# A new order table for a 16-token-tile adaLN linear-attention and MLP block on one core

## The chip, the cores and the metric

The kernel runs on one core of one Trainium2 chip. The metric is the time of one execution on the device in microseconds (us); the median of several executions is given. Engines are named as the profile names them: PE is TensorE's matmul, PEld its weight load, DVE is VectorE, ACT is ScalarE, POOL is GpSimd, and SP is SyncE, whose queue issues nearly all the DMAs here.

## The reference

There are 2048 tokens of width 576, 32 heads of width 18, and an MLP of width 4608. All arrays are float32.

```python
mod = (silu(c) @ w_mod)                      # six rows of 576: sa, ca, ga, sb, cb, gb
h = layernorm(x) * (1 + ca) + sa
q, k, v = h @ wqkv                           # per head
phi = lambda t: where(t > 0, t + 1, exp(t)) + 1e-6
kv, z = sum_s phi(k) v, sum_s phi(k)         # over all tokens
o = phi(q) kv / (phi(q) z + 1e-6)
x = x + ga * (o @ wo)
h = layernorm(x) * (1 + cb) + sb
out = x + gb * (silu(h @ w1) @ w2)
```

## The kernel before

The tokens lie in 16 tiles of 128, in four blocks of four. Every matmul operand is kept as a rounded part and a rest ("hi" and "lo"), so that a product takes three matmuls instead of one: hi times hi, lo times hi, hi times lo. ScalarE makes the hi part as a copy (`w_hi`, `split_h`, `scaled_hi`), and VectorE makes the rest as a difference of two tiles in SBUF (`sub_hi` on L262, `scaled_lo` on L268). This is why VectorE and GpSimd have so much to do.

The program has these stages, each with its span in the profile:

- **First projections** (0 to about 24 us): the modulation row from `c`, and K of the first two token tiles.
- **K and Q** (24 to about 210 us): for each block of four tiles LayerNorm, the transposed and modulated activations `hT` (rest parts on L262 for the first block and L998 for the others), K and phi(K) (`psK`, L929), partial products with the rows of x (`psG`, L1054; VectorE adds them into `sum` on L1064), Q for most tiles, and the second and third part of the modulation rows (GpSimd sums `tmod`, L1104). Then the state `kv` and its product with `wo` (L1224).
- **Attention output and the second LayerNorm** (210 to about 357 us): `big`, L390 and L1358; the transposes of the normalised rows into `small` (L375) and their hi and lo parts; beside it a first MLP slice in a plain form, `small` L1433 up and `big` L1444 down, whose results VectorE adds into the output rows `acc` (L1449).
- **MLP** (357 to the end): the remaining slices, in which seven products replace eight (a Strassen scheme over 2x2 blocks of tokens, hidden columns and outputs). An up product (`up`, L1925) is taken out of PSUM by VectorE on L1947 and L1949 and by ScalarE, GpSimd forms sums and differences of the results (L1960 to L1967), hi and lo parts are made (L1983, L1987), and the down products (`down`, L2009) are added to `acc` and to helper rows `U` by VectorE (L2018 to L2022). The weights are prepared in the same way: GpSimd sums (L1575 to L1583), hi parts, lo parts (L262, L268).

How the order of the work is set: the code first writes down the operations stage by stage (`STAGE_A` orders the K and Q stage while it is written down; the rest of the MLP is written down by the small scheduler `Schedule.emit`). At the end, `arrange(ORDERS, begun)` (L252, called on L2380) goes through the table `ORDERS`, which has one list of numbers for each engine. Number n is the n-th instruction that was written down for that engine after `begun`; the list says in which order the engine runs them, and each instruction is tied to the one before it in the list. What is not in a list follows in the order in which it was written. The lists hold the first 2991 of the 6939 matmuls and transposes, 656 instructions of VectorE, 486 of ScalarE, 258 of GpSimd and 203 DMAs on SP's queue. This covers the program until about 470 us of the profile; the steady part of the MLP behind it is in no list.

An engine runs its list strictly in order: when one instruction waits, all behind it wait too. The waits themselves come from the data and from buffers that are used again. A PSUM bank can be written again only when VectorE or ScalarE has read it out.

```python
ORDERS = {                                   # L67
    "PE": """ 0-43 45-46 52 49-50 ... """, "DVE": ..., "Activation": ..., "Pool": ..., "SP": ...
}
def arrange(orders, start):                  # L252
    for engine, text in orders.items():
        traced = [i for i in nc.cur_bb.bb.instructions[start:] if i.engine == ... and listed(i)]
        order = [j for part in text.split() for j in span(part)]
        order += sorted(set(range(len(traced))) - set(order))
        for a, b in zip(order, order[1:]):
            follow(traced[b], traced[a])
```

Of the kernel before, what the change touches and what calls it, by code (L numbers as in the profile page):

```python
# [24 lines left out]
def kernel(ctx: ExitStack, tc, A_x, A_wqkv, A_wo, B_x, B_w1, B_w2, c, w_mod, out):  # L25
# [33 lines left out]
    def behind(instructions):  # L59

        with ExitStack() as order:
# [8 lines left out]
            116 84-87 90-91 124 88-89 92-105 117 106-111 125 118-123 112-115 126-141 154-173 142-147 174-177  # L70
            148-153 210-217 178-179 246-249 180-181 250-251 290-291 182-201 218-221 256-267 274-289 202-209
            292-295 302-319 222-227 320-329 228-237 268-273 330-331 296-299 332-335 300-301 336-337 238-245
            252-255 342-343 338-341 344-353 366-367 354-365 368-391 412-413 398-403 392-395 414-423 396-397
            406-411 424-425 436-439 426-427 440-445 404-405 446-451 428-435 452-457 462-463 458-461 464-517
            524-527 518-519 530-533 520-523 534-553 572-573 586-587 574-575 554-571 588-591 598-601 528-529
            592-595 602-609 596-597 610-629 576-579 630-645 580-585 646-653 658-661 682-685 662-669 686-687
            692-697 688-689 698-701 654-657 670-673 690-691 702-703 674-681 704-763 770-771 764-769 772-787
            826-829 788-825 838-843 862-865 830-833 844-845 866-867 846-857 872-875 834-837 890-891 876-877
            892-893 878-889 894-901 858-861 868-871 926-931 902-925 932-943 950-951 944-945 952-963 946-949
            978-983 1000-1001 966-977 984-999 1002-1015 1022-1027 1016-1021 1028-1029 964-965 1030-1075  # L80
            1084-1085 1076-1077 1102-1117 1086-1093 1130-1135 1118-1119 1078-1079 1120-1121 1136-1137 1122-1129
            1138-1139 1080-1083 1140-1145 1094-1095 1160-1161 1096-1101 1146-1157 1172-1177 1162-1171 1158-1159
            1248-1249 1178-1183 1250-1253 1184-1185 1254-1257 1186-1199 1208-1213 1258-1259 1285-1286 1200-1207
            1287-1292 1214-1219 1236-1237 1220-1227 1238-1247 1228-1235 1293-1300 1260-1284 1301-1339 1352-1356
            1340-1351 1357-1386 1413-1417 1387-1412 1418-1439 1446-1450 1440-1445 1451-1488 1507-1510 1489-1494
            1511-1513 1495-1506 1514-1558 1573-1576 1601-1604 1559-1572 1605 1577-1586 1634 1638 1587-1600
            1606-1623 1646-1649 1624-1625 1650 1655-1660 1626-1633 1661-1670 1639 1635-1637 1640-1641 1687-1688
            1671-1678 1715-1719 1679-1680 1642-1643 1681-1682 1651 1689-1694 1652-1653 1644-1645 1695-1698 1654
            1699-1710 1720-1727 1711-1712 1728-1731 1713-1714 1683 1748 1684-1685 1732-1745 1749 1686 1746-1747
            1776-1779 1781-1784 1780 1762 1785-1790 1763-1765 1791-1792 1750 1793-1798 1751-1761 1766-1771  # L90
            1799-1802 1772-1775 1854 1803-1809 1821-1825 1870 1810 1855-1857 1811 1826-1827 1812-1813 1871-1873
            1828-1831 1874-1876 1832-1835 1877 1836-1839 1814-1816 1858-1860 1883-1886 1817-1819 1861-1862 1820
            1840-1843 1863-1864 1844-1853 1865-1868 1915-1918 1869 1878-1882 1887-1904 1976 1990 1977-1980
            1919-1921 1905-1906 1922-1926 1991 1981 1907-1908 1931-1934 1982 1909-1914 1983-1984 1927-1930 1985
            1935 1992 1936-1941 1986 1942-1947 1987-1989 1948-1967 1993-1995 1968-1972 2004-2010 1973-1975
            2011-2022 1996-1999 2023-2028 2000 2029-2036 2001-2003 2037-2038 2049-2069 2039-2048 2070-2081 2086
            2082 2098-2099 2087-2088 2106-2110 2089-2095 2100-2101 2083-2085 2096-2097 2115-2136 2102 2137-2142
            2147 2159-2160 2103-2105 2111-2113 2161-2162 2148 2114 2187-2190 2163-2166 2149 2143-2146 2167-2168
            2150 2169-2186 2151 2191 2199 2192-2194 2200-2202 2152-2153 2203-2210 2195 2213 2211-2212 2154-2158
            2196-2198 2214-2224 2231-2234 2225-2230 2239 2249 2259-2261 2240 2235-2238 2262 2245 2241-2242  # L100
            2246-2247 2243 2255-2258 2248 2244 2265-2270 2295 2263 2250-2254 2271 2264 2272-2274 2296-2298
            2283-2284 2299-2305 2285-2287 2309 2288-2291 2277-2278 2292-2293 2310-2311 2275-2276 2312-2313 2294
            2306-2308 2279-2282 2314-2323 2329-2333 2335 2324 2336-2339 2334 2347-2352 2340 2353-2354 2325-2328
            2355-2358 2341 2359-2363 2342 2364-2365 2343-2344 2366-2369 2345-2346 2370-2375 2377 2376 2378-2382
            2391-2398 2383-2387 2399 2388-2389 2400-2402 2390 2403-2407 2427-2428 2408-2412 2421 2433 2413-2420
# [2306 lines left out]
```

## Time and profile before

| | us |
|---|---|
| median of 3 runs (lowest, highest) | 1093.39 (1093.04, 1094.13) |
| the profiled execution, its own time | 1092.31 |
| span of the profile, first to last instruction | 1090.6 |
| PE busy in the span | 1064.8 (98%) |
| DVE busy | 913.4 (84%) |
| POOL busy | 741.3 (68%) |
| ACT busy | 708.5 (65%) |

The profiled execution took 1.7 us more than its span, and 1.08 us less than the median. A busy PE is a PE with a matmul in flight; idle time of the other engines costs nothing where PE doesn't wait for them. So what matters is where PE is idle, and which engine ends each wait.

### The profile page before, as it was taken

The numbers are of one execution on the slowest core, as the hardware profiler recorded it, in microseconds if no ns is written. First come the engines' busy times: TensorE is split into PE (matmuls) and PEld (weight loads), VectorE is DVE, ScalarE is ACT, GpSimd is POOL, SyncE is SP. The second block draws the span as 40 slices with busy tenths as digits, with TensorE's granted clock in tenths as the row PEclk, the third lists the DMA queues.
The fourth block names the chain that finished last, engine by engine and source line by source line (L and its number), as shares of the span: only waits on it lengthen the run. The fifth ranks groups of instructions, "written<-read, shape, count | busy, mean of one in ns | idle before, by whom it ended". The sixth has DMA issues, their size and how long they took to land.

```text
span 1090.6 us, 19057 instructions
## 1 busy us (share of the span) xinstructions
PE 1064.8 (98%) x7027; PEld 758.6 (70%) x7027; DVE 913.4 (84%) x1438; ACT 708.5 (65%) x1318; POOL 741.3 (68%) x804
## 2 busy tenths in 40 slices
PE   8899999999999899999999999999999999999998
PEld 6899999899785455666666666666666666666665
DVE  7968968778889799998997888987987887898767
ACT  5766554246757686677667767776776776676554
POOL 3556615655725499879878778877788678677563
PEclk9999999999999999999999999999999999999999
DMA  9497665223256768478577667567657747616522
GB/s 292 123 214 174 64 182 130 54 81 106 66 183 224 206 239 249 136 229 247 176 204 244 172 194 224 197 207 221 201 168 254 206 137 264 208 63 201 169 79 109
DMA packets 119342, 193.51 MB, mean 177 GB/s; under 512 B 42892, under 2 KB 77584, under 8 KB 119248
## 3 DMA queue, kind: packets, MB, share of 16 engines
q1 hardware_dynamic: 86276, 190.81, 56.2%
q10 hardware_dynamic: 32972, 1.48, 3.1%
q8 instruction: 55, 0.90, 0.3%
q14 instruction: 39, 0.32, 0.1%
HBM read 176.77 MB, written 15.48 MB: 176 GB/s over the span
## 4 chain that ended last, share of the span: by engine, by line
PE 77%; DVE 12%; ACT 3%; DMA 3%; issue 3%; POOL 2%; SPq 0%; DVEq 0%; POOLq 0%; ACTq 0%
PE up L1925 30%; PE down L2009 29%; PE big L390 6%; PE psK L929 4%; PE psG L1054 3%; DVE hT L262 1%; PE small L1433 1%; PE big L1444 1%; PE psK L1224 1%; DVE acc L1021 1%; DMA hT<-in_B_w_dram 1%; DMA turned<-acc 1%; PE big L1358 1%; DVE w L262 1%; DMA hT<-in_w_mod_dram 1%
## 5 line engine op out<-in xcount | busy, mean ns | idle before, releaser
L1925 PE MATMUL up<-hT,w 128*128 128x512 f16 x1264 | 317.6, 379 | 2.6 <-ACT p L1900 1.6
L1925 PEld LDWEIGHTS <-w 128*128 128x128 f16 x1492 | 146.0, 98 | 140.0 <-issue 3.9
L2018 DVE SCALAR_TENSOR_TENSOR acc<-acc,set,down 128x576 f32<-128x576 f32 x128 | 103.4, 810 | 31.4 <-PE down L2009 30.5
L1943 ACT ACTIVATE f<-f,set 128x512 f32<-128x512 f32 x102 | 73.0, 718 | 59.7 <-DVE f L1949 50.4
L1963 POOL TENSOR_TENSOR s<-f,f 128x256 f32<-128x256 f32 x66 | 55.2, 836 | 73.2 <-ACT f L1944 70.8
L2009 PE MATMUL down<-w,hc 128*128 128x288 f16 x600 | 90.8, 286 | 0.4 <-ACT f L1939 0.4
L2009 PE MATMUL down<-w,hb 128*128 128x288 f16 x600 | 90.5, 286 | 0.2 <-DVE acc L2018 0.2
L2009 PE MATMUL down<-w,hT 128*128 128x288 f16 x480 | 82.9, 286 | 0.4 <-DVE acc L2022 0.4
L1947 DVE TENSOR_TENSOR f<-up,p 128x512 f32<-128x512 f32 x102 | 69.6, 682 | 15.1 <-PE up L1925 8.6
L1944 ACT ACTIVATE f<-f,set 128x512 f32<-128x512 f32 x102 | 73.6, 722 | 3.2
L2009 PEld LDWEIGHTS <-hb 128*128 128x128 f16 x600 | 58.7, 98 | 22.6 <-issue 0.7
L2009 PEld LDWEIGHTS <-hc 128*128 128x128 f16 x600 | 58.6, 98 | 22.5 <-DVE acc L2018 0.7
L1949 DVE TENSOR_TENSOR f<-up,f 128x512 f32<-128x512 f32 x68 | 46.9, 689 | 26.6 <-PE up L1925 25.5
L1987 POOL TENSOR_TENSOR hc<-s,hc 128x512 f16<-128x512 f32 x50 | 63.7, 1274 | 6.4 <-ACT hc L1983 6.4
L1967 POOL TENSOR_TENSOR f<-f,s 128x256 f32<-128x256 f32 x66 | 53.6, 812 | 18.5 <-DVE hb L1987 10.2
L1960 POOL TENSOR_TENSOR s<-f 128x256 f32<-128x256 f32 x66 | 55.9, 847 | 14.1 <-ACT f L1940 11.3
L2009 PEld LDWEIGHTS <-hT 128*128 128x128 f16 x480 | 46.9, 98 | 26.6 <-issue 0.8
L390 PE MATMUL big<-w,qT 128*128 128x288 f32 x352 | 59.6, 307 | 0.6 <-DVE acc L1372 0.6
L1965 POOL TENSOR_TENSOR s<-s,f 128x256 f32<-128x256 f32 x66 | 56.4, 854 | 3.6
L2009 PE MATMUL down<-w,ha 128*128 128x288 f16 x396 | 55.6, 286 | 0.3 <-DVE w L262 0.3
L2009 PE MATMUL down<-w,hd 128*128 128x288 f16 x396 | 55.5, 286 | 0.2 <-ACT hd L1983 0.2
L1987 POOL TENSOR_TENSOR hd<-s,hd 128x256 f16<-128x256 f32 x66 | 50.5, 765 | 6.6 <-ACT hd L1983 6.6
(408 smaller groups left out, 2830.1 us busy)
## 6 DMA issues: line engine op xcount, KB each, us to landing
hT<-hd SPq DMA_DIRECT2D x101, 640.0 KB, 5.2
hT<-hd SPq DMA_DIRECT2D x65, 512.0 KB, 3.9
hT<-in_B_w_dram SPq DMA_DIRECT2D x14, 576.0 KB, 5.1
hT<-in_B_w_dram SPq DMA_DIRECT2D x28, 256.0 KB, 6.4
raw<-in_B_w_dram SPq DMA_DIRECT2D x11, 576.0 KB, 4.4
v<-in_B_w_dram SPq DMA_DIRECT2D x9, 576.0 KB, 5.1
acc<-in_A_x_dram SPq DMA_DIRECT2D x16, 288.0 KB, 5.0
raw<-in_B_w_dram SPq DMA_DIRECT2D x9, 512.0 KB, 5.6
```

Source lines behind the costliest of these rows:

```text
L390: T.matmul(ps, xpart(a), wpart(b), start=n == 0, stop=n == len(XW) - 1)
L1925: T.matmul(ps, left, right, start=first and m == 0, stop=m == len(seq) - 1, skip_group_check=True)
L1943: A.activation(f, f, AF.Silu, scale=factor(self.g, "inv"))
L1944: A.activation(f, f, AF.Identity, scale=factor(self.g, "delta"))
L1947: V.tensor_add(f, self.bank[bank[1]], self.p1)
L1960: G.tensor_sub(self.s3, half(i, 0, 0), half(i, 0, 1))
L1963: G.tensor_add(self.s[:, 0:1], half(i, 0, 1), half(i, 1, 1))
L1965: G.tensor_sub(self.s[:, 1:2], self.s[:, 0:1], half(i, 0, 0))
L1967: G.tensor_sub(half(i, 1, 0), half(i, 1, 0), self.s[:, 1:2])
L1987: eng.tensor_sub(t[:, :, 1, :], src, t[:, :, 0, :])
L2009: T.matmul(ps[:, p, :HALF], left[:, u, p * P : (p + 1) * P], right[:, v], start=n in (1, 5, 7, 6) and j == 0, stop=j == len(passes) - 1, s ...
L2018: V.scalar_tensor_tensor(dst, dst, factor(self.g, "ratio"), ps[:, :, :HALF], op0=ALU.mult, op1=ALU.add)
```

## The change

The diff replaces the five lists of `ORDERS` by five other lists over the same numbers (ScalarE's list takes in three instructions more, GpSimd's four). Nothing else is touched: the same instructions with the same operands run on the same engines, and the tables of `STAGE_A` and the scheduler are as before. [...] The changed file has one line less in the table, so that in its listings every line number behind the table is lower by one (L998 of before is L997).

The first two rows of PE's list, cut to their beginning, show how the table reads:

```diff
     ORDERS = {
         "PE": """
             0-43 45-46 52 49-50 44 47-48 53-54 51 65 57-58 61-62 66-72 55-56 59-60 63-64 73-77 82-83 80-81 78-79
-            116 84-87 90-91 124 88-89 92-105 117 106-111 125 118-123 112-115 126-141 154-173 142-147 174-177
+            84-87 90-91 88-89 92-101 116-118 102-103 124 104-105 119-123 125 106-115 126-141 154-167 142-153
...
```

Up to its 84th instruction PE runs as before (until 24.9 us of the profile). Of the 6939 instructions of PE 2536 stand at another place, of VectorE's 543 of 1438, of ScalarE's 392, of GpSimd's 227 and of SP's 161. Most moves are short: the farthest ones on PE are 64 places forward and 77 back. Behind the lists the order of all engines is the same. Three places show what moved.

VectorE between 99 and 116 us of the profile, where it makes the rest parts `hT` of the third block from the block's rows in `acc_93` and `h_119` (L998; L362 modulates them first), and adds a partial product into `sum_109` (L1064). Before:

```order
L1064 TENSOR_TENSOR sum_108<-psG_116,sum_108 128x576
L942 TENSOR_SCALAR acc_92<-psK 128x576
L495 SCALAR_TENSOR_TENSOR acc_92<-e,acc_92 128x576
L362 TENSOR_SCALAR acc_93<-acc_93,col_a 128x512 x2
L1064 TENSOR_TENSOR sum_109<-psG_117,sum_109 128x576
L998 TENSOR_TENSOR hT<-acc_93,hT 128x4x4x32 x2
L942 TENSOR_SCALAR acc_92<-psK 128x576
L998 TENSOR_TENSOR hT<-acc_93,hT 128x4x4x32
L337 BN_STATS st<-acc_94 128x6 x2
L998 TENSOR_TENSOR hT<-h_119,hT 128x4x4x32
L998 TENSOR_TENSOR hT<-acc_93,hT 128x4x4x32
```

The same stretch of VectorE's instructions in the changed kernel:

```order
L1063 TENSOR_TENSOR sum_108<-psG_116,sum_108 128x576
L1063 TENSOR_TENSOR sum_107<-psG_117,sum_107 128x576
L336 BN_STATS st<-acc_94 128x6 x2
L337 BN_AGGR mv<-st 128x2
L336 BN_STATS st<-acc_94 128x6
L941 TENSOR_SCALAR acc_92<-psK 128x576 x2
L361 TENSOR_SCALAR acc_93<-acc_93,col_a 128x512
L997 TENSOR_TENSOR hT<-acc_93,hT 128x4x4x32
L361 TENSOR_SCALAR acc_93<-acc_93,col_a 128x512
L1063 TENSOR_TENSOR sum_109<-psG_117,sum_109 128x576
L336 BN_STATS st<-acc_94 128x6 x2
L997 TENSOR_TENSOR hT<-acc_93,hT 128x4x4x32 x3
```

The statistics of the next block (BN_STATS, one input) moved ahead; the first addition of L495 and the rest part of `h_119` moved behind the last three of the four parts from `acc_93`.

VectorE at the end of the attention stage, 354 to 361 us: the four additions of the last plain down products (`big`, each with its own bank number) into `acc3`, between weight splits (`w_3657`) and the activations `S`. Before:

```order
L1449 SCALAR_TENSOR_TENSOR acc3_94<-acc3_94,set0_99,big_3888 128x576
L262 TENSOR_TENSOR S_3672<-S_3670,S_3672 128x512
L1449 SCALAR_TENSOR_TENSOR acc3_94<-acc3_94,set0_99,big_3895 128x576
L262 TENSOR_TENSOR S_3672<-S_3670,S_3672 128x512
L268 SCALAR_TENSOR_TENSOR w_3657<-v_3658,set0_99,w_3657 128x256
L1449 SCALAR_TENSOR_TENSOR acc3_94<-acc3_94,set0_99,big_3923 128x576
L268 SCALAR_TENSOR_TENSOR w_3657<-raw_3660,set0_99,w_3657 128x256
L1449 SCALAR_TENSOR_TENSOR acc3_94<-acc3_94,set0_99,big_3881 128x576
L268 SCALAR_TENSOR_TENSOR w_3657<-v_3658,set0_99,w_3657 128x256 x2
L268 SCALAR_TENSOR_TENSOR w_3657<-raw_3660,set0_99,w_3657 128x256
```

The same place in the changed kernel:

```order
L1448 SCALAR_TENSOR_TENSOR acc3_94<-acc3_94,set0_99,big_3888 128x576
L261 TENSOR_TENSOR S_3672<-S_3670,S_3672 128x512
L267 SCALAR_TENSOR_TENSOR w_3657<-v_3658,set0_99,w_3657 128x256
L1448 SCALAR_TENSOR_TENSOR acc3_94<-acc3_94,set0_99,big_3881 128x576
L1448 SCALAR_TENSOR_TENSOR acc3_94<-acc3_94,set0_99,big_3895 128x576
L267 SCALAR_TENSOR_TENSOR w_3657<-raw_3660,set0_99,w_3657 128x256
L1448 SCALAR_TENSOR_TENSOR acc3_94<-acc3_94,set0_99,big_3923 128x576
L267 SCALAR_TENSOR_TENSOR w_3657<-raw_3660,set0_99,w_3657 128x256
```

The addition of `big_3881`, last of the four before, is now the second; the first up product of the MLP waits for it before, and for the addition of `big_3895` in the changed kernel. The two splits of `w_3657` that stood behind the four additions now stand ahead of these rows.

VectorE at about 435 to 441 us, in the MLP, where `w22`, `w24` and `w27` are the rest parts of a weight slice for the down products, `hb0` and `hb1` those of two activations, and `f01` an up product. Before:

```order
L1987 TENSOR_TENSOR hb0_4087<-f01_4633,hb0_4087 128x2x256
L262 TENSOR_TENSOR w24_3971<-S_3808,w24_3971 128x288
L748 TENSOR_TENSOR set1_100<-set1_100,set0_99 128x1
L2018 SCALAR_TENSOR_TENSOR U0_3978<-U0_3978,set1_100,down_4772 128x576
L262 TENSOR_TENSOR w22_3970<-v_3658,w22_3970 128x288
L262 TENSOR_TENSOR w27_3969<-S_3808,w27_3969 128x288
L2022 TENSOR_TENSOR acc3_94<-down_4688,acc3_94 128x2x288
L262 TENSOR_TENSOR w27_3969<-v_3658,w27_3969 128x288
L262 TENSOR_TENSOR w22_3970<-raw_3982,w22_3970 128x288
L1987 TENSOR_TENSOR hb1_4064<-f11_4673,hb1_4064 128x2x256
L1947 TENSOR_TENSOR f01_4853<-up_4791,p1_4788 128x512
```

The same place in the changed kernel:

```order
L1946 TENSOR_TENSOR f10_4755<-up_4589,p1_4586 128x512
L1986 TENSOR_TENSOR hb0_4087<-f01_4633,hb0_4087 128x2x256
L2017 SCALAR_TENSOR_TENSOR U0_3978<-U0_3978,set1_100,down_4772 128x576
L261 TENSOR_TENSOR w22_3970<-raw_3982,w22_3970 128x288
L261 TENSOR_TENSOR w27_3969<-v_3658,w27_3969 128x288
L261 TENSOR_TENSOR w27_3969<-S_3808,w27_3969 128x288
L1946 TENSOR_TENSOR f01_4853<-up_4791,p1_4788 128x512
L1986 TENSOR_TENSOR hb1_4064<-f11_4673,hb1_4064 128x2x256
L2021 TENSOR_TENSOR acc3_94<-down_4688,acc3_94 128x2x288
```

The second half of `w22` moved ahead of two other weight splits and of the addition into `acc3`. On PE, the products that read it moved ahead too: of what PE runs before the fifth of them, 19 up products with `w`, one with `wta` and 12 down products with `hd` now come behind it.

More of the change, by code (lines that the diff above doesn't have):

```diff
@@ L74 @@
[L74 to L88, printed above, removed]
```

198 lines of the change are left out of this document (106 added, 92 removed).

## The prediction

> **What bounds the kernel now.** I first read the busy times of the engines on the page:
>
> ```profile
> PE 1064.8 (98%) x7027; PEld 758.6 (70%) x7027; DVE 913.4 (84%) x1438; ACT 708.5 (65%) x1318; POOL 741.3 (68%) x804
> ```
>
> PE is in use for 98% of the span, so an order can give back at most PE's idle time. Where that lies is read from the busy times by stretch; the stretches are cut where PE's idleness changes (columns: stretch, its length, busy us and instructions of PE, PEld, DVE, ACT, POOL, granted clock, DMA).
>
> ```profile
> 0.00:24.00 24.00, 20.24 (x123) 15.82 (x123) 17.09 (x46) 11.14 (x22) 8.99 (x13) 1.00 0.94 303
> 24.00:60.00 36.00, 32.31 (x236) 31.31 (x237) 31.69 (x51) 28.58 (x45) 18.61 (x15) 1.00 0.49 138
> 60.00:100.00 40.00, 40.00 (x302) 40.00 (x302) 28.74 (x46) 25.18 (x36) 21.73 (x16) 1.00 0.99 200
> 100.00:126.00 26.00, 22.73 (x166) 21.86 (x165) 24.83 (x34) 15.02 (x23) 19.32 (x13) 1.00 0.35 107
> 126.00:170.00 44.00, 43.51 (x328) 43.24 (x327) 32.39 (x42) 26.60 (x46) 14.30 (x10) 1.00 0.81 140
> 170.00:210.00 40.00, 38.71 (x268) 36.01 (x268) 29.75 (x47) 10.39 (x17) 22.91 (x19) 1.00 0.33 82
> 210.00:270.00 60.00, 60.00 (x457) 58.76 (x456) 48.53 (x101) 32.10 (x52) 35.30 (x34) 1.00 0.32 92
> 270.00:300.00 30.00, 28.14 (x195) 22.45 (x194) 26.95 (x41) 22.28 (x37) 22.04 (x19) 1.00 0.31 84
> 300.00:340.00 40.00, 39.72 (x288) 32.27 (x288) 35.91 (x75) 24.56 (x40) 13.30 (x14) 1.00 0.55 189
> 340.00:378.00 38.00, 33.77 (x183) 17.76 (x182) 31.82 (x47) 24.59 (x48) 15.12 (x16) 0.96 0.70 220
> 378.00:410.00 32.00, 31.01 (x187) 18.00 (x185) 30.37 (x45) 26.68 (x56) 29.93 (x37) 1.00 0.68 239
> 410.00:470.00 60.00, 58.43 (x362) 34.63 (x360) 58.90 (x91) 41.05 (x86) 51.28 (x63) 1.00 0.60 182
> 470.00:1050.00 580.00, 580.00 (x3702) 361.98 (x3701) 488.46 (x741) 399.75 (x788) 446.19 (x521) 1.00 0.63 197
> 1050.00:1090.60 40.60, 36.18 (x254) 24.52 (x251) 28.00 (x43) 20.54 (x33) 22.30 (x21) 1.00 0.27 101
> ```
>
> Length less PE's busy time gives the idle time. From 470 to 1050 us there is none, so whatever the lists gain or lose is fixed by about 470 us and carried to the end. The first 24 us (3.76 idle) and the last 40.6 us (4.42) are outside the lists. Between lie 3.69 + 0 + 3.27 + 0.49 + 1.29 + 0 + 1.86 + 0.28 + 4.23 + 0.99 + 1.57 = 17.67 us of idle time: the whole prize. Where PE idles, VectorE is almost always the engine near its limit (24.83 of 26 us, 26.95 of 30, 30.37 of 32, 58.90 of 60).
>
> Second, what holds VectorE up. Durations of one form, as minimum, median and maximum in ns:
>
> ```profile
> L1947 DVE TENSOR_TENSOR f<-up,p x102: 672/678/692, 364.2 to 1072.4; 128x512 f32<-128x512 f32 x102
> L998 DVE TENSOR_TENSOR hT<-acc,hT x12: 678/691/1956, 69.3 to 153.5; 128x512 fp32r<-128x512 f32 x12
> ```
>
> L1947 reads one operand from PSUM and is the same each time, L998 reads two tiles in SBUF and takes up to 1.28 us more for the same work. At 100 to 116 us the two engines stand side by side like this (start, us):
>
> ```profile
> 101.46 1.20 DVE L495 SCALAR_TENSOR_TENSOR acc<-e,acc 128x576 f32<-128x576 f32 x1
> ...
> 106.38 3.08 DVE L998 TENSOR_TENSOR hT<-acc,hT 128x512 fp32r<-128x512 f32 x2
> 110.05 1.96 DVE L998 TENSOR_TENSOR hT<-acc,hT 128x512 fp32r<-128x512 f32 x1
> 112.65 2.42 DVE L998 TENSOR_TENSOR hT<-h,hT 128x512 fp32r<-128x512 f32 x1
> 115.00 0.68 DVE L998 TENSOR_TENSOR hT<-acc,hT 128x512 fp32r<-128x512 f32 x1
> 115.60 0.45 DVE L337 BATCH_NORM_STATS2 st<-acc 128x6 f32<-128x288 f32 x1
> ...
> 102.12 3.39 POOL L1104 TENSOR_TENSOR tmod<-tmod,acc 128x576 f32<-128x576 f32 x2
> 110.02 3.27 POOL L1104 TENSOR_TENSOR tmod<-tmod,raw 64x576 f32<-64x576 f32 x2 [1.11 <-issue]
> ```
>
> The L998 issued at 110.05, beside GpSimd's pair, ends at 112.0: some 0.7 us, its clean time, after the first of the pair (half of 3.27) is done. The one at 112.65, while the second still runs, takes 2.42. So with two operands in SBUF VectorE waits for GpSimd's turn to end. [...]
>
> **The change part by part.** Nothing is added or removed, so each term is a place where a wait of PE gets longer or shorter. I count the work that stands ahead of the instruction that ends a wait, and the PE work ahead of the one that waits, in both orders.
>
> *100 to 126 us (3.27 idle).* Two waits make up most of it:
>
> ```profile
> PE psK L929 <- DVE hT L998: 1.6, 1, 1.6
> PE psG L1054 <- DVE sum L1064: 1.3, 1, 1.3
> ```
>
> The first ends with the L998 at 115.00. In the changed order two of the rows above leave its front, the addition on L495 (1.20) and the part of `h_119` (2.42), 3.6 us as they ran; three statistics and an aggregate take their place, 3 x 0.45 and at most as much again, so 1.4 to 1.8 us is won. PE's work ahead of the one that waits grows by two matmuls, 0.13 us each (302 in 40.00 us from 60 to 100). So the L998 comes about 2 us earlier than now, if the conflicts that left are not replaced; the wait of 1.6 would be gone. For the second wait the sum on L1064 gets the three statistics, one more L998 (0.68) and one more L942 ahead of it and loses the L495: some 2 us of clean work more. PE has 24 more matmuls to run before it needs the sum, 3.1 us, so that stays covered. I take half of the two waits and a little: they hang on conflicts that only partly go. **Taken: -1.7**; bounds -3.3 (both waits go) and +1.7 (the conflicts only change partners and the sum is late).
>
> *340 to 378 us (4.23 idle).* The largest single wait:
>
> ```profile
> 359.70 4.44 PE L1925 MATMUL up<-first,w 128*128 128x512 f16 x12 [2.08 <-ACT S L1632]
> 357.66 0.81 DVE L1449 SCALAR_TENSOR_TENSOR acc<-acc,set,big 128x576 f32<-128x576 f32 x1 [0.31 <-PE big L1444]
> 358.39 0.48 DVE L268 SCALAR_TENSOR_TENSOR w<-raw,set,w 128x256 f16<-128x256 f32 x1
> 358.79 0.81 DVE L1449 SCALAR_TENSOR_TENSOR acc<-acc,set,big 128x576 f32<-128x576 f32 x1
> 360.00:363.00 3.00, 3.00 (x9) 1.08 (x8) 0.79 (x2) 0.28 (x1) 1.69 (x2) 0.50 0.57 171
> ```
>
> The profile names ScalarE, but its `S` was done; by time the fourth addition of L1449, which ends at 359.60 and frees the bank, lets PE go 0.10 later. In the changed order PE waits for the third of the four; the fourth and one split (0.81 + 0.48) come behind it, but two splits (0.9) were pulled ahead of it, so VectorE reaches it only some 0.3 us sooner. VectorE has no slack here (0.31 idle in the rows), so I take 0.3, not the 2.1 of the wait. Right behind the wait the clock stood at 0.50 and twelve matmuls took 4.44 us instead of 12 x 0.216 = 2.6 (rows of the chain of waits further down), a further 1.8 us. With a shorter gap that may go; I count 0.8 for it. **Taken: -1.1**; bounds -4.2 - 1.8 = -6.0, and +1.0 (the first reading of `up` on L1947 now has two `S` differences ahead of it that were behind it, each like the 0.68 of L998 above). [...]
>
> *24 to 60, 126 to 210 and 270 to 340 us* (3.69 + 0.49 + 1.29 + 1.86 + 0.28 = 7.61 idle). The same kinds of instructions are shuffled over at most some tens of places; I found no such clear removal. I take a quarter, half of the share taken at 100 us: **-1.9**; bounds -7.6 and +3.2 (at 50 us PE's products for the second K pair were moved 3.4 us ahead, VectorE's rest part for them 1.1 us back, with 1.3 us between them now).
>
> *378 to 470 us (2.56 idle).* VectorE and GpSimd together have 89.27 + 81.21 us of busy time in 92 us. At 440 us:
>
> ```profile
> 436.27 0.45 DVE L262 TENSOR_TENSOR w<-S,w 128x288 f16<-128x288 f32 x1
> 436.64 0.75 DVE L2022 TENSOR_TENSOR acc<-down,acc 128x576 f32<-128x576 f32 x1
> ...
> 438.60 0.98 DVE L262 TENSOR_TENSOR w<-raw,w 128x288 f16<-128x288 f32 x1
> 440.29 1.14 PE L2009 MATMUL down<-w,hb 128*128 128x288 f16 x8
> ```
>
> What PE's products cost is read from the chain of waits (start, us, what):
>
> ```profile
> 445.01 1.74 PE up L1925 x8
> ...
> 477.43 1.47 PE down L2009 x12
> ```
>
> That is 0.216 us for an up product and 0.122 for a down product. PE's product at 440.29 follows VectorE's split, which ends at 439.58, by 0.7 us. The new lists take 20 up products and 12 down products from in front of it, 5.8 us, but from in front of the split only three others (0.45 each), one addition (0.75), with four tiny steps added: 1.2 us. If VectorE went on at its pace, PE would wait 5.8 - 1.2 - 0.7 = 3.9 us. It will not be quite that if VectorE loses less to GpSimd until there. **Taken: 0**; bounds -2.6 and +3.2 (3.9, less 0.7 us for such waits as PE has behind 440 us now, an estimate: a share of the 1.57 from 410 to 470).
>
> *60 to 100 and 210 to 270 us*: PE is never idle, 0. SP's queue:
>
> ```profile
> 354.00 2.74 DMA hd<-S
> hT<-hd SPq DMA_DIRECT2D x101, 640.0 KB, 5.2
> ```
>
> The fetch of `first` for that first up product moved behind two stores of `hd`. These wait for an `S` of VectorE, and one went out at 354.00. Issued then, the fetch lands at 359.2, 0.5 before PE starts now: 0, while VectorE is no later.
>
> The sum is -1.7 - 1.1 - 1.9 + 0 = -4.7 us. The profiled execution took 1092.31 (span 1090.6 and 1.7 around it), 1.08 below the median; it goes to 1087.6, and the median from 1093.39 to **1088.7**.
>
> **The rivals.** (1) *The MLP's start waits for VectorE.* [...] It decides when VectorE's overrun between 378 and 440 us falls by less than the 3.9 - 0.7 = 3.2 us. With the earlier gains at 0 the time is 1093.4 + 3.2 = 1096.6. For it: 58.90 of 60; against: earlier gains, if any, arrive as slack. (2) *More of it works*: two thirds of the idle time goes, 0.67 x 17.7 = 11.8: 1081.6. For it: every large wait but ScalarE's ends in VectorE, with overrun ahead. (3) *The conflicts only change places*, and the orders are equal on the chip: 1093.4. [...] (4) *The first K tiles get out of step*: +3.2 at 50 us, with nothing back: 1096.6, the same side as (1).
>
> **How the numbers follow.** Forecast 0.40, (1) 0.27, (2) 0.15, (3) 0.12, (4) 0.06. Faster by over 0.2% (2.2 us, about what a measurement of this kernel can tell from no change): 0.40 + 0.15 = 0.55; within: 0.12; slower: 0.33. The range goes from 1077 (most of the prize of 17.7 and some of the clock's 1.8 us) to 1100 (both slower rivals together, 3.2 + 3.2). The forecast's own range is 1083 to 1091.
>
> **What would show it.** Right: between 100 and 116 us the last L997 part ends some 2 us earlier against PE's work and PE's wait for it is under 0.5 us; the wait before the first `up` is under 2 us and no row has the clock at 0.50; PE's idle time from 24 to 470 us is near 13 us. Wrong: PE waits over 1 us for the split of `w22` (L261) near 435 us, or VectorE's overrun is as large as before, or PE is idle beyond 470 us.

## The result and the profile after

The changed kernel took 1085.44 us (median of 4 runs, 1081.64 to 1086.77), the kernel before 1093.76 beside it; the ratio is 0.9919, 95% interval 0.9893 to 0.9944, which is 8.9 us (6.1 to 11.7). Two further sets of runs of the same lists gave 1083.84 and 1085.29. The forecast was 1088.7.

The busy times by the same stretches, for the changed kernel (columns as before):

```profile
PE 1063.3 (98%) x7027; PEld 760.6 (70%) x7027; DVE 893.0 (82%) x1438; ACT 707.3 (65%) x1318; POOL 737.6 (68%) x804
```

```profile
0.00:24.00 24.00, 19.75 (x105) 15.26 (x105) 16.46 (x41) 10.17 (x19) 7.74 (x13) 0.93 0.95 314
24.00:60.00 36.00, 34.48 (x251) 32.99 (x251) 30.80 (x55) 28.56 (x47) 19.62 (x14) 1.00 0.54 164
60.00:100.00 40.00, 40.00 (x304) 40.00 (x303) 27.30 (x47) 25.47 (x36) 24.45 (x17) 1.00 0.98 193
100.00:126.00 26.00, 25.35 (x191) 25.10 (x189) 21.73 (x36) 18.14 (x29) 19.98 (x14) 1.00 0.55 90
126.00:170.00 44.00, 43.37 (x326) 43.14 (x326) 27.52 (x42) 23.77 (x40) 17.84 (x16) 1.00 0.72 148
170.00:210.00 40.00, 38.07 (x266) 35.55 (x265) 29.15 (x54) 10.32 (x16) 17.40 (x15) 1.00 0.30 78
210.00:270.00 60.00, 59.70 (x448) 56.95 (x446) 48.48 (x94) 34.09 (x56) 31.48 (x33) 1.00 0.36 111
270.00:300.00 30.00, 29.07 (x214) 24.76 (x213) 26.25 (x47) 20.34 (x33) 20.59 (x18) 1.00 0.25 72
300.00:340.00 40.00, 39.47 (x279) 31.43 (x279) 35.26 (x69) 26.60 (x44) 16.14 (x17) 1.00 0.56 181
340.00:378.00 38.00, 32.64 (x191) 18.18 (x189) 33.31 (x51) 26.95 (x55) 19.41 (x26) 1.00 0.75 216
378.00:410.00 32.00, 31.41 (x188) 18.27 (x187) 30.54 (x49) 23.36 (x48) 26.83 (x32) 1.00 0.78 250
410.00:470.00 60.00, 59.51 (x372) 35.99 (x370) 55.26 (x89) 43.89 (x90) 50.87 (x62) 1.00 0.58 187
470.00:1050.00 580.00, 580.00 (x3708) 362.56 (x3706) 486.26 (x738) 399.50 (x788) 448.06 (x522) 1.00 0.63 196
```

PE's idle time from 24 to 470 us is 12.93 us instead of 17.67. It shrank in five stretches (24 to 60: 3.69 to 1.52; 100 to 126: 3.27 to 0.65; 270 to 300: 1.86 to 0.93; 378 to 410: 0.99 to 0.59; 410 to 470: 1.57 to 0.49). It grew by 1.33 in all in four others (126 to 270 and 300 to 340), and from 340 to 378 from 4.23 to 5.36, where time was nevertheless gained by the clock (1.00 here, 0.96 before; below). From 470 to 1050 us PE is never idle, as before. VectorE did the same instructions in 893.0 us instead of 913.4.

Stretches of the clock on the wall don't hold the same work in two kernels. So I also compare by work: each PE instruction counts with the usual distance from its start to the next one's, and where the old order has done so much work at time t, the table says how much later (+) or earlier (-) another kernel has done as much. `again` and `again2` are the changed lists once more; `till130` and `from325` follow below.

| at t of before (us) | after | again | again2 | till130 | from325 |
|---|---|---|---|---|---|
| 24 | +3.0 | +0.5 | +0.4 | +2.0 | +0.2 |
| 60 | +0.5 | -1.7 | -0.2 | -1.0 | +0.2 |
| 100 | +0.3 | -1.8 | -0.3 | -1.7 | +0.1 |
| 126 | -2.9 | -4.3 | -3.8 | -5.0 | +0.2 |
| 340 | -3.0 | -4.5 | -4.0 | -4.9 | +0.7 |
| 360 | -2.8 | -4.3 | -3.8 | -5.0 | +2.1 |
| 370 | -4.4 | -6.0 | -5.5 | -6.6 | +0.4 |
| 390 | -3.8 | -7.6 | -5.4 | -7.0 | -0.1 |
| 470 | -5.8 | -9.5 | -7.6 | -6.9 | -2.4 |

So the gain is made at three places: 24 to 60 us (2.5, 2.2 and 0.6 in the three profiles), 100 to 126 (3.2, 2.5, 3.5), and 340 to 470 (2.8, 5.0, 3.6). From 126 to 340 us there is none in sum: 0.9 to 1.0 us are lost up to 270 us, and 1.2 to 1.3 won from there to 300 us. The 3.0 us at the start of the first profile are lost in a part where both tables have the same order on PE, VectorE and ScalarE.

Place by place, first 97 to 114 us. The rows of VectorE and GpSimd of the changed kernel:

```profile
105.24 1.92 DVE L997 TENSOR_TENSOR hT<-acc,hT 128x512 fp32r<-128x512 f32 x1
110.06 1.87 DVE L997 TENSOR_TENSOR hT<-acc,hT 128x512 fp32r<-128x512 f32 x3
111.85 0.74 DVE L494 SCALAR_TENSOR_TENSOR acc<-z,acc 128x576 f32<-128x576 f32 x1
112.52 0.68 DVE L997 TENSOR_TENSOR hT<-h,hT 128x512 fp32r<-128x512 f32 x1
...
106.58 1.88 POOL L1103 TENSOR_TENSOR tmod<-tmod,acc 128x576 f32<-128x576 f32 x1
108.53 1.48 POOL L1103 TENSOR_TENSOR tmod<-tmod,raw 64x576 f32<-64x576 f32 x1
112.63 2.67 POOL L977 TENSOR_TENSOR xs<-xt,xs 128x512 fp32r<-128x512 f32 x1 [2.61 <-ACT xs L975]
```

GpSimd is through with its sums at 110.0 us (113.3 before) and then idle for 2.6 us. In just that gap VectorE runs three parts of `hT` in 1.87 us, 0.62 each, and the part of `h_119` in 0.68 (2.42 before). GpSimd's next operation, on L977, pays instead: it takes 2.67 us, where the same operation took 1.29 before. The last of the parts from `acc` ends at 111.9 us instead of 115.7. PE's longest waits from 24 to 126 us are now:

```profile
PE psG L1053 <- DVE sum L1063: 0.7, 1, 0.7
PE psG L567 <- DVE col_a L532: 0.6, 1, 0.6
PE psK L928 <- ACT e L935: 0.5, 1, 0.5
```

The 1.6 for `hT` is gone, and the 1.3 for the sum is 0.7. So are the two waits of 1.3 between 24 and 60 us: one for a rest part on L262 that ended at 44.8 us (1.28), one for ScalarE's `z` that ended at 52.8 us (1.33).

Second, 340 to 378 us, PE's waits in order of time:

```profile
342.47 1.88 PE L1443 MATMUL big<-w,hs 128*128 128x288 f16 x14 [1.87 <-DVE acc L1448]
350.76 5.44 PE L1443 MATMUL big<-w,hs 128*128 128x288 f16 x43 [0.45 <-DVE hs L267]
356.99 1.67 PE L1924 MATMUL up<-first,w 128*128 128x512 f16 x7 [0.78 <-DVE acc L1448]
374.17 1.47 PE L1924 MATMUL up<-hT,w 128*128 128x512 f16 x6 [2.17 <-DMA hT<-hd]
```

The wait before the first `up` fell from 2.08 to 0.78, and the products behind it take 1.67 us for 7, at a clock of 1.00, where 12 took 4.44, with the clock at 0.50 for 3.41 us of it. In exchange the new lists have a wait of 1.87 for an addition of L1448 at 342 us that the old ones had not, and PE, now earlier, waits for a fetch of `hT` at 374 us.

So the wait was moved, not removed: 1.87 + 0.45 + 0.78 = 3.10 us stand where 0.44 + 0.26 + 0.18 + 2.08 = 2.96 stood, and from 340 to 360 us the new lists win nothing (the table has +0.2 in each of the three profiles). The 1.6 to 1.7 us that they win from 360 to 370 us are the clock. `till130` shows it: it has the old order here and the same wait of 2.08, but its clock stayed at 1.00, its 12 products took 2.75 us instead of 4.44, and it wins 1.6 us there as well:

```profile
354.77 2.75 PE L1921 MATMUL up<-first,w 128*128 128x512 f16 x12 [2.08 <-ACT S L1628]
```

From 370 to 390 us the three profiles of the new lists differ (0.6 us lost, 1.6 won, none), with the wait that they meet there: 2.17 for the fetch of `hT` in the first, 0.35 for it in the second, 1.7 for a `w` of ScalarE in the third.

Third, the split of `w22`. VectorE and PE:

```profile
428.20 0.69 DVE L261 TENSOR_TENSOR w<-raw,w 128x288 f16<-128x288 f32 x1
...
428.57 1.63 PE L2008 MATMUL down<-w,hb 128*128 128x288 f16 x12
```

The split came at 428.2 instead of 438.6 us and PE's product at 429.06 instead of 440.29 (the fifth of the run of twelve is the one that reads it). PE doesn't wait, by a margin of 0.16 us. VectorE was not behind its work here: 0.7 us ahead of the split it had itself waited 0.28 us for a down product of PE.

### The profile page after: what moved, and what is told of

Same layout as the page of the kernel before. It is cut to its first block, busy times and chain, and to the rows that moved or that the text cites. A ratio compares the mean times of both kernels' runs of the same rounds, so it can differ in the third digit from the quotient of the medians.

```text
span 1085.1 us, 19052 instructions
## 1 busy us (share of the span) xinstructions
PE 1063.3 (98%) x7027; PEld 760.6 (70%) x7027; DVE 893.0 (82%) x1438; ACT 707.3 (65%) x1318; POOL 737.6 (68%) x804
## 3 DMA queue, kind: packets, MB, share of 16 engines
q10 hardware_dynamic: 32972, 1.48, 3.1%
## 4 chain that ended last, share of the span: by engine, by line
PE 80%; DVE 9%; DMA 4%; ACT 2%; POOL 2%; issue 1%; SPq 0%; DVEq 0%; POOLq 0%; ACTq 0%
PE up L1924 31%; PE down L2008 30%; PE big L389 5%; PE psK L928 4%; PE psG L1053 4%; PE big L1443 2%; DMA raw<-parts 1%; DMA hT<-hd 1%; PE small L1432 1%; DVE hT L261 1%; PE small L374 1%; DMA raw<-in_w_mod_dram 1%; DVE w L261 1%; PE big L1357 1%; PE psK L1223 1%
## 5 line engine op out<-in xcount | busy, mean ns | idle before, releaser
L1946 DVE TENSOR_TENSOR f<-up,p 128x512 f32<-128x512 f32 x102 | 69.6, 682 | 13.8 <-PE up L1924 9.4
L1966 POOL TENSOR_TENSOR f<-f,s 128x256 f32<-128x256 f32 x66 | 53.4, 809 | 17.3 <-DVE hb L1986 10.2
L1053 PE MATMUL psG<-w,xs 128*128 128x288 f32 x336 | 52.2, 296 | 1.3 <-DVE sum L1063 1.3
```

Source lines behind the costliest of these rows:

```text
L1053: T.matmul(ps[:, h, :HALF], l, pk[t][:, u, h * HALF : (h + 1) * HALF], start=t == 0 and m == 0, stop=t == 3 and m == len(left) - 1)
L1946: V.tensor_add(f, self.bank[bank[1]], self.p1)
```

## The experiments

The theory: the new lists gain by letting VectorE lose less to GpSimd ahead of PE's waits. The rival: they gain by the order of the work alone, more of PE's work ahead of each wait and the additions that free PE's banks in a better sequence, whoever blocks VectorE. "Overrun" means: for all VectorE instructions from 20 to 480 us, the sum of what each takes longer than the shortest one of the same line, operation and shape in the profile of the kernel before. It was 84.7 us before and is 63.4 after (65.3 and 65.0 in the two repetitions). Lines of these kernels are shifted by up to 10 against before.

**The lists again**, twice, without an edit.

> The changed lists once more. In the first profile of them PE was 3.0 us late at 24 us, in a part of the program that both tables order alike, and 8.8 us ahead of the old lists from there to 470 us. Chance: the pair of L518 and the L261 at 16 to 19 us meet GpSimd's L475 only when a fetch lands early, so this profile may have PE on time at 24 us, with a span near 1082; PE's idle time from 24 to 470 us stays at 9 to 12 us, and the runs go from 1081 to 1087. Rival, that the new lists make the start late themselves: PE is 2 to 3 us late at 24 us in this profile too.

> The changed lists as they are, beside the three others on one chip: 1082.5 to 1085.5, median 1083.8, if the spread of 1081.6 to 1086.8 seen so far comes from halvings of the clock that some executions have and others not.

Measured: 1083.84 (1083.04 to 1084.48, 6 runs; ratio 0.9916, 0.9902 to 0.9930) and 1085.29 (1082.90 to 1087.13, 5 runs; 0.9926, 0.9913 to 0.9939). PE was 0.5 and 0.4 us late at 24 us, so the late start is chance, and the new lists alone don't bring it about. PE's idle time from 24 to 470 us was 12.0 us in the first, at the end of what was expected, and 12.3 in the second.

**Stages apart.** `till130` takes the new order for all that the changed kernel starts before 130 us, and then the old one; `from325` the old order for what the kernel before starts ahead of 325 us, and then the new one.

```diff
-"PE": the new list
+"PE": 825 numbers of the new list, then the rest as in the old list        (till130; the other engines in the same way)
+"PE": 2166 numbers of the old list, then the rest as in the new list       (from325)
```

> The new lists for what the changed kernel begins before 130 us, then the old order. If the gain of each stage stays in it (24 to 60 us: 2.6, 100 to 126 us: 3.3): 1093.6 - 5.9 = 1087.7, up to 3 more when the start is late as in the first profile of the new lists. Rival, that PE coming early only waits longer for VectorE behind 130 us: 1091 to 1093.6, with PE's idle time from 130 to 470 us up by 3 us or more.

> The old order for what the kernel before begins ahead of 325 us, then the new lists. If each stage has its own gain (about 0.8 from 340 to 390 us and 2.0 from 390 to 470 us): 1093.6 - 2.8 = 1090.8. Rival, that the late stages gain because VectorE and GpSimd come into them earlier relative to PE: 1093.6 within 1. Rival of the prediction, that the MLP's start waits for VectorE: 1096.8, with a wait of over 1 us for L262 near 435 us.

Measured: till130 1088.03 against 1092.16 (0.9958, 0.9945 to 0.9971), which is -4.6 us; from325 1090.06 against 1092.16 (0.9977, 0.9966 to 0.9989), -2.5 us. The table above shows till130 at -5.0 at 126 us and still -4.9 at 340: early gains are not eaten. The idle time from 130 to 470 us was 9.7 us, less than the 10.7 before, so that rival falls. Together the two give 7.1 of the 8 to 9 us. The MLP's start gains with the old order ahead of it too, 3.1 us from 340 to 470 us in the table; rival (1) of the prediction falls, there is no wait at all for the split near 435 us.

**Two rows alone.** In the old list of VectorE the addition of L495 (146) and the part of `h_119` (150) move behind the last part of `acc_93` (149), the two rows that the prediction counted.

```diff
-144 146 143 142 141 145 147 151 148 152 156 150 149 153
+144 143 142 141 145 147 151 148 152 156 149 146 150 153
```

> The old lists, in which only two rows of VectorE move: the addition of L495 at 101.5 us and the part of h_119 at 112.65 us go behind the last of the three parts of acc_93 (115.00 us). The step of the prediction: 3.6 us leave the front of the part that PE waits for at 115.7 us, which then comes 1.5 to 3.6 us earlier, and PE's wait of 1.6 goes: 1092.0. Rival, that the parts then meet GpSimd's sums in other places and come no earlier: 1093.6 within 0.5, with the wait still over 1 us.

Measured: 1091.25 against 1092.16 (0.9988, 0.9976 to 0.9999), -1.3 us, an interval that ends just short of nothing. VectorE and GpSimd of this kernel:

```profile
110.27 1.19 DVE L994 TENSOR_TENSOR hT<-acc,hT 128x512 fp32r<-128x512 f32 x1
111.38 3.20 DVE L491 SCALAR_TENSOR_TENSOR acc<-e,acc 128x576 f32<-128x576 f32 x1
114.50 0.68 DVE L994 TENSOR_TENSOR hT<-h,hT 128x512 fp32r<-128x512 f32 x1
...
109.14 3.59 POOL L1100 TENSOR_TENSOR tmod<-tmod,raw 64x576 f32<-64x576 f32 x2
112.70 1.26 POOL L974 TENSOR_TENSOR xs<-xt,xs 128x512 fp32r<-128x512 f32 x1
```

The last part of `acc_93` ends at 111.5 us, 4.2 earlier; 1.5 to 3.6 had been expected. But the addition that was moved behind it now meets GpSimd, and takes 3.20 us, where it took 1.20 before and 0.74 undisturbed. The part of `h_119` stands behind it, and PE waits for that one:

```profile
115.24 0.53 PE L925 MATMUL psK<-v,hT 128*128 128x288 f32 x2 [1.90 <-DVE hT L994]
```

So for `hT` the conflict only changed its victim: the wait is 1.90 instead of 1.57. What this run won is the other wait, the 1.27 for the sum on L1064. The addition of L495 had stood ahead of that sum as well, which now starts 1.7 us earlier (104.0 instead of 105.7 us), and PE no longer waits for it. The step is right for what it counted, and too short: the whole group of instructions has to get past GpSimd's sums, which the new lists do by bringing the sums forward too.

**The sums out of the way.** GpSimd's sums of `tmod` on 8 of 576 columns, in the old lists and in the new.

```diff
-G.tensor_add(dst[:, a], dst[:, a], raw[:, a])
+G.tensor_add(dst[:, a][:, :8], dst[:, a][:, :8], raw[:, a][:, :8])
```

> The old lists; GpSimd's sums of tmod (L1104) take 8 of the 576 columns, so that they are short (the second and third part of the modulation rows come out wrong). If these sums are what makes the parts of hT and the sum late at 103 to 116 us: the waits of 1.6 and 1.3 us there go, VectorE's overrun from 100 to 120 us falls from 8.1 to under 3, and the time is 1092.2 - 2.9 = 1089.3. Rival, that PE's order there has too little work ahead of the two waits whatever VectorE does: over 1.5 us of wait stay, and the time is 1091.5 or more.

> The new lists with GpSimd's sums of tmod (L1104) on 8 of 576 columns (the modulation rows come out wrong). In the old lists the same edit gave 4.3 us. If the new lists have won at 100 to 126 us by dodging these sums, little is left to win: 0 to 1.8 us (PE's idle time there is 0.7 to 1.8 us), 1082 to 1084. Rival, that they won by the order of PE's work: the sums still cost what they cost in the old lists, 3 us or more, so 1080.5 or less.

Measured: in the old lists 1088.11 against 1092.45 (0.9959, 0.9943 to 0.9976), -4.5 us; in the new ones 1082.40 against 1093.01 (0.9909, 0.9893 to 0.9925), 1.4 to 3.0 below the three medians of the new lists, and 2.9 below the one on the same chip. The time is in the range that was given for dodging (1082 to 1084), but the difference lies between the 1.8 of that reading and the 3 of the rival, so this run does not decide by its time. The stretch from 100 to 126 us, of the old lists and of the new, with this edit:

```profile
100.00:126.00 26.00, 25.78 (x197) 25.56 (x196) 22.22 (x39) 17.62 (x27) 10.89 (x11) 1.00 0.50 120
```

```profile
100.00:126.00 26.00, 25.50 (x192) 25.27 (x191) 20.32 (x37) 19.04 (x30) 8.38 (x13) 1.00 0.48 115
```

With PE's order unchanged, its idle time there falls from 3.27 to 0.22 us once the sums are short. At this place the wait is all the doing of GpSimd's sums. In the new lists only 0.5 us were left to win there (0.50 idle against 1.05 in `again2`). VectorE's overrun from 100 to 120 us in the old lists fell only to 4.5, not under 3, which was enough. The 4.5 us are more than this place has: PE's idle time from 24 to 60 us fell too, from 3.69 to 1.60.

**GpSimd reads nothing.** All its sums, differences and products write a constant into the same output instead, in the old lists and in the new; its few small powers on 128x4 elements stay.

```diff
+class Blank:
+    def __getattr__(self, name):
+        if name in ("tensor_add", "tensor_sub", "tensor_mul"):
+            return lambda out, a, b: nc.gpsimd.memset(f32(out) if out.dtype == F32R else out, 0.5)
+        return getattr(nc.gpsimd, name)
+G = Blank()
```

> The old lists; every sum, difference and product of GpSimd writes a constant into its output instead of reading two tiles, so GpSimd's work is there but shorter and reads nothing (the output is not the reference's). If GpSimd's reads are what VectorE loses its time to: VectorE's overrun from 20 to 480 us falls from 84.7 to under 25, PE's idle time from 24 to 470 us from 17.7 to under 9, the time to 1083 or less, no more than 2.5 us from that of the new lists with the same edit. Rival, that the old order keeps PE waiting by its order alone, whoever blocks VectorE: overrun falls, but PE's idle time stays over 12 and the time over 1087.

> The new lists with the same edit: GpSimd writes constants and reads nothing. If the new lists gain by dodging GpSimd, the edit has little left to give: 1080 to 1083, within 2.5 us of the old lists with the edit. Rival, gain by the order alone: 6 us or more below the old lists with the edit, so 1078 or so against 1087.

Measured: 1076.64 (1074.42 to 1081.20) with the old lists and 1071.24 (1069.73 to 1074.94) with the new, 4 runs each; 0.9851 (0.9823 to 0.9880) and 0.9802 (0.9775 to 0.9828) against before. The overrun fell from 84.7 to 13.8 us, and from 63.4 to 10.3. For the operation of L998, as minimum, median and maximum in ns, in the old lists with the edit:

```profile
L1005 DVE TENSOR_TENSOR hT<-acc,hT x12: 678/684/692, 68.0 to 145.1; 128x512 fp32r<-128x512 f32 x12
```

The maximum was 1956. So most of the overrun goes when GpSimd's reads go, but the two orders still lie 5.4 us apart (about 4.2 either way, both intervals taken together). 2.5 was the bound for the theory alone, and 6 the least for the rival: the median lies between, and with that interval the times decide for neither. PE's idle time from 24 to 470 us is 9.6 us with the old lists, over the 9 of the theory and under the 12 of the rival, and 3.3 with the new. The stretches in which they differ most, and that from 100 to 126 us, of the old lists and then of the new:

```profile
24.00:60.00 36.00, 33.88 (x256) 33.27 (x256) 29.48 (x51) 29.02 (x48) 10.51 (x19) 1.00 0.50 146
...
100.00:126.00 26.00, 26.00 (x201) 26.00 (x200) 19.61 (x42) 18.18 (x29) 5.27 (x9) 1.00 0.55 100
...
340.00:378.00 38.00, 33.73 (x182) 17.69 (x181) 26.74 (x48) 26.30 (x54) 8.14 (x29) 0.96 0.75 241
...
410.00:470.00 60.00, 57.98 (x355) 35.20 (x353) 42.18 (x86) 42.04 (x88) 18.99 (x67) 0.97 0.57 182
```

```profile
24.00:60.00 36.00, 35.94 (x269) 35.32 (x270) 27.16 (x60) 29.35 (x49) 9.38 (x16) 1.00 0.66 198
...
340.00:378.00 38.00, 36.06 (x208) 19.99 (x206) 30.27 (x56) 30.68 (x63) 9.75 (x36) 1.00 0.83 253
...
410.00:470.00 60.00, 60.00 (x382) 37.15 (x380) 43.76 (x86) 43.84 (x89) 18.87 (x64) 1.00 0.62 195
```

In the old lists 2.12 us stay idle from 24 to 60 us and 4.27 from 340 to 378, which is all that was there before (4.23); in the new lists 0.06 and 1.94. The 2.12 are two waits of the kinds that the kernel before has there (1.38 for a rest part, 0.74 for `z`), with nobody blocking VectorE, and the new lists with the edit have neither: that gain is order. From 410 to 470 us the old lists with the edit wait 2.02 us for a fetch of `hT`, and the mean clock there is 0.97; the new ones don't wait, and it is 1.00. The wait before the first `up` in the old lists with the edit:

```profile
348.74 4.44 PE L1932 MATMUL up<-first,w 128*128 128x512 f16 x12 [2.07 <-ACT S L1639]
```

2.07 us, as in the kernel before, with nobody blocking VectorE; and 0.78 in the new lists with the edit. So the order of the additions, which is the rival's, decides how long this wait is. But only with the edit does it win the time: the wait of 1.87 at 342 us is gone there, so that one is GpSimd's doing, and without the edit it takes back what the order gives. Between 100 and 126 us the old order has no wait left with the edit: that gain is the theory's. The edit also takes away what GpSimd waits for and most of its time (5.27 us are left of 19.32 from 100 to 126 us). So 100 to 126 us is won by dodging, 24 to 60 us at least in part by order, and 360 to 370 us by the clock (from 340 to 378 us 1.00 in the new lists and 0.96 in the old). Which of the two wins the 2 us from 390 to 470 us, and how the 8 to 9 us divide in all, these runs don't show.

**The late start.** In the first profile of the new lists GpSimd's L475 and the L676 behind it met VectorE's L518 and L261 at 16 to 20 us (the pair took 2.84 us, the L261 1.48). Here GpSimd's five numbers at 13 to 27 us change places so that they can't.

```diff
-5 7 6 8 4
+7 6 5 8 4
```

> The new lists, with five rows of GpSimd at 13 to 27 us in another order: the rest part of xs first, then the power for the LayerNorm, and only then the rest part of v, which met L518 and L261 of VectorE at 16 to 19 us in the first profile of the new lists. If that meeting is what made the start late by 2 to 3 us in some executions: the pair of L518 takes 1.8 us and the L261 0.42, PE is within 0.5 us of the old lists at 24 us, and the median falls by about 1 us to 1083 with a smaller spread. Rival, that the part of v or xs then comes late or meets others: a wait of PE or VectorE before 36 us grows, and the median stays at 1083.8 or rises.

Measured: 1085.62 (1083.98 to 1087.70; 0.9923, 0.9902 to 0.9945), no gain. The meeting was gone (the pair 1.80 us, the L261's kind 0.42), and still PE was 2.0 us late at 24 us, because the clock was halved in this profile:

```profile
16.00:18.00 2.00, 2.00 (x8) 1.64 (x9) 1.96 (x4) 0.67 (x1) 0.00 (x0) 0.50 1.06 376
18.00:20.00 2.00, 2.00 (x4) 0.09 (x2) 1.78 (x7) 0.00 (x0) 0.04 (x1) 0.50 1.07 327
```

And PE waited 1.9 us for a part of `hT` at 75.9 us, which it did in none of the three profiles of the new lists. My cause for the late start was wrong, or only a part of it.

**The new wait at 342 us.** The addition of L1448 (I-3792, number 489 in VectorE's list) goes two rows or one row ahead.

```diff
-476 485 486 489 475 487
+476 489 485 486 475 487        (swap_a)
+476 485 489 486 475 487        (swap_b)
```

> The new lists with one row moved: the addition of L1449 (I-3792) that PE waits 1.9 us for near 341 us goes two rows ahead of where the new lists have it, in front of the differences L1685 and L1686, though the product it adds comes 0.6 us after VectorE could begin. If the new lists only put a wait of VectorE's making there: the wait falls to under 0.3 us and the time by 1.5 to 2 us, to 1082. Rival, that the chain of L1685 to L1687 then brings S, and the store and fetch of it, late for the first up products: the wait comes back between 350 and 378 us and the time stays at 1083.8 within 0.7.

> The same addition goes one row ahead, between L1685 and L1686, so that VectorE doesn't idle for it: the wait of 1.9 us falls to about 0.8 and the time by 1.1 us, to 1082.7. Rival as before: it comes back behind, 1083.8 within 0.7.

Measured, beside 1085.29 for the new lists on the same chip: 1085.90 (1084.48 to 1087.48) and 1084.48 (1082.52 to 1085.37). In the first, PE's longest waits from 330 to 390 us are:

```profile
PE big L1439 <- DVE acc L1444: 1.9, 2, 1.5
PE up L1920 <- DMA hT<-hd: 0.9, 1, 0.9
PE up L1920 <- DVE acc L1444: 0.8, 1, 0.8
```

The wait of 1.9 left 342 us and came back at 350 us as 1.5 and 0.4 for additions behind it, and from 351.27 us 42 products of `big` took 6.99 us, where 43 took 5.44 in the changed kernel. That is 1.7 us more, as much as a stretch of 3.41 us at half clock costs (an estimate from these numbers). VectorE doesn't idle in its rows from 339.95 to 346.4 us, and the row that goes ahead makes the others late. That is the rival. In swap_b the wait splits into three, 1.8 us together; its time can't be told from that of the new lists, and no version beat them clearly.

## Why the prediction came out right, step by step

- **The prize and its place** were right: everything was won before 470 us and carried to the end.
- **100 to 126 us, taken -1.7**: right in kind, too small in size; 2.5 to 3.5 us were won, nearly the whole bound of -3.3. I took half because "they hang on conflicts that only partly go". They went almost wholly (0.7 to 1.8 us of idle time are left in the three profiles), and not by the two rows that I counted: `two_rows` won 1.3 us, and that at the wait for the sum. GpSimd's sums came 3.3 us earlier as well, a move on an engine whose list I had not read for this place. Two workings were off. 3.6 us less the 1.35 to 2.7 that I set against them is 0.9 to 2.3, not 1.4 to 1.8; against PE's work the last part came 3.3 us earlier. And the part at 112.65 us didn't wait for the second sum alone, which ended at 113.29 us: it ended at 115.08, behind GpSimd's L978 as well (113.24 to 114.53).
- **340 to 378 us, taken -1.1** (0.3 for the wait, 0.8 for the clock, my estimate from the 1.8 us that its half cost): the wait before `up` shrank by 1.3, not 0.3, because the addition that PE waits for was no longer last of the four. That won nothing, because of the wait of 1.87 at 342 us, which I did not see: up to 360 us the new lists are 0.2 us behind. The clock's share came in full, 1.6 to 1.7 us, against a profile that had it. From 340 to 390 us the three profiles won 0.8, 3.1 and 1.4. Their mean is 1.8, so the term came out near it, but not as it was added up: the 0.3 brought nothing and the 0.8 was half of what the clock gave.
- **24 to 60 us and the rest, taken -1.9**: 24 to 60 us alone won 0.6 to 2.5, the rest nothing in sum; right as a sum, and that is luck, for the quarter that I took came from no row. The fear of rival (4), that the first K pair gets out of step, did not come true: no wait over 0.5 us near 50 us.
- **378 to 470 us, taken 0**: 1.9 to 2.2 us were won from 390 to 470 us. The rival (1) was to decide by VectorE's overrun from 378 to 440 us falling by less than 3.2 us. It fell from 15.2 to 11.5, 11.4 and 11.5 us in the three profiles, 3.7 to 3.9, and the split came in time, by 0.16 us. I counted work ahead and held the overrun fixed, in a place where the overrun changed. That the fall in overrun is what won the 2 us is not shown.
- **Sum**: -4.7 forecast, -8.9 measured (6.1 to 11.7), nearly twice as much. The direction and the places hold; the terms for 100 to 126 us and for 378 to 470 us were too small by about 1.4 and 2 us, that for 340 to 378 us by 0.7. Of the signs named for "right", PE's idle time near 13 us (12.93), the last L997 part some 2 us earlier (3.3), the wait before `up` under 2 us and no row there at clock 0.50 are all there; the wait for `hT` at 100 to 116 us is gone in the first and third profile and 0.51 in the second, at its bound. None of the signs for "wrong" is there.

## What to carry to other kernels

When two engines hold each other up, count the instructions of both around a wait: moving the blocked one ahead hands the block to the row behind it (in `two_rows` the wait for `hT` was 1.90 us instead of 1.57), and what helps is that the blocker is through before the group begins (the part of `h_119` then took 0.68 us instead of 2.42). A wait for one of several results (here four additions) is first a question of which comes last, and is settled without any engine getting faster (here 0.78 us instead of 2.08). Before a term is sized from one profile, ask what in that profile was chance: here the start, up to 3.0 us, and a halved clock, 1.6 to 1.7 us. And a wait that shrinks is no gain before the waits ahead of it are read too: here 1.3 us less at one place were 1.87 more at another.

## What the runs showed of the hardware that was not expected

**The half clock came in stretches of 3.41 us, from 26 us on after little work of PE.** In the trace's record of the granted clock the kernel before has one stretch at 0.50 ahead of its last microsecond, from 359.90 us, and the changed kernel has one, from 20.83 us; each lasts 3.413 us. The half clock at the very end begins 214.0 such lengths after that start in the one and 312.0 in the other, while the two starts, counted in such lengths, differ by a fraction of 0.35. So each of the two records fits a grid of its own. By the rows of 2 us, the stretch at 0.50 at the start is 6.8 us long in `till130` and `early_pool` and 10.2 us in `tmod_b`, about two and three times as long. The window ahead of the half clock, and that one, of the kernel before:

```profile
356.50:359.90 3.40, 1.32 (x11) 0.79 (x9) 3.09 (x6) 2.06 (x4) 0.00 (x0) 1.00 0.59 211
359.90:363.30 3.40, 3.40 (x9) 1.22 (x8) 0.89 (x3) 0.58 (x2) 1.69 (x2) 0.50 0.51 154
```

And of till130, the same old order of this place. Counted in lengths of 3.41 us from its half clock at the start (15.7 us by the same rows), a new window begins at 353.6 us, amid the wait:

```profile
350.20:353.60 3.40, 2.50 (x21) 1.76 (x18) 3.09 (x6) 1.68 (x4) 0.00 (x0) 1.00 0.69 243
353.60:357.00 3.40, 2.23 (x11) 1.07 (x12) 2.26 (x5) 0.90 (x3) 1.31 (x2) 1.00 0.46 152
357.00:360.40 3.40, 3.40 (x18) 1.51 (x17) 2.40 (x4) 2.70 (x7) 0.39 (x1) 1.00 0.50 127
```

Of the windows of 3.413 us on these grids that begin between 26 and 470 us at full clock, in the record of before the only one with less than 1.84 us of PE work is the one above, and only behind it was the clock halved; in that of the changed kernel the least is 1.61 (from 372.37 us), and the clock was not halved. In single rows of other runs, a clock of 0.51 follows 1.27 us (`tmod_b`, 424.8 to 428.2 us) and 1.50 us (`two_rows`, 113.1 to 116.5 us). `again` has the nearest miss of these rows, 1.54 (the rows are cut to 3.40 us):

```profile
338.30:341.70 3.40, 1.54 (x11) 0.93 (x10) 3.31 (x4) 2.68 (x7) 3.34 (x5) 1.00 0.71 220
341.70:345.10 3.40, 3.40 (x22) 1.97 (x21) 3.37 (x5) 0.56 (x1) 1.41 (x2) 1.00 0.03 7
```

Ahead of 26 us the clock also fell after more: in the changed kernel after 1.79 us of PE work (17.4 to 20.8 us), and in till130, whose half clock starts at 15.7 us, PE was busy for 3.41 of the 4 us from 12 to 16 us. With the old order before the first `up` (a wait of 2.08 us before and in till130, 2.07 in blank_b) the mean clock from 340 to 378 us was 0.96 in four profiles (before, two_rows, tmod_b, blank_b) and 1.00 in till130; with the new order (a wait of 0.78 in the changed kernel and in blank_a) it was 1.00 in all four that have this row (after, again, early_pool, blank_a). So a wait of 2.1 us came with a half clock in some executions and not in others. The nearest miss above is the new lists' wait of 1.9 at 342 us, with 0.04 us more of PE work than the window of two_rows behind which the clock was halved.

The spread between runs goes with the mean clock. Of 57 runs of the kernel before, the 12 with a mean clock of 1.000 took 1089.6 to 1091.9 us (median 1090.9), the 16 with 0.995 or less 1092.0 to 1099.1 (1093.4). Of the 15 of the new lists, the 5 at 1.000 took 1081.6 to 1083.8 (1083.0) and the others 1083.9 to 1087.1. At full clock the new lists gain 7.9 us.

**With GpSimd's large reads gone, VectorE's difference never took over 693 ns.** GpSimd's writes of a constant were still there (with its few other operations 5.27 us of busy time from 100 to 126 us in the old lists with the edit, 5.90 in the new). L998's operation took 678 to 693 ns in all its fifteen instructions in the old lists and 676 to 692 in the new, where it took up to 2.42 us before.
